# Feed-forward per 128-token block, whole-sequence loads into 64-float slots, and weights held behind the first loads, in a gated linear attention plus MLP kernel

## Chip, cores, metric

One core of one Trainium2 chip. The metric is device time in microseconds, the median of several executions. A ratio is the mean time of one kernel's fast runs over that of the other's fast runs of the same rounds, so it is not quite the ratio of the medians quoted. The profiled span is about 2 us shorter than the time.

## The reference

```python
# q, k, v, f_logit: [4, 8, 768, 48] fp32 (batch, heads, sequence, head dim)
f = 1 / (1 + exp(-f_logit))
for t in range(S):
    state = f[:, :, t, :, None] * state + einsum('bhd,bhe->bhde', k[:, :, t], v[:, :, t])
    y[:, :, t] = einsum('bhd,bhde->bhe', q[:, :, t], state)
x = y.transpose(0, 2, 1, 3).reshape(3072, 384)
h = x @ w_in                      # [384, 2048]
out = softplus(h) @ w_out         # [2048, 384]
```

The recurrence is done in 24 blocks of 128 tokens, six to a sequence.

## The kernel before

Each block of q, k, v and f_logit is loaded by itself: a partition is a token, and its 8 heads are 8 runs of 192 B in DRAM. All weights are issued early, from GpSimd (POOL), and arrive as bf16 (3.15 MB on that queue, q0 of the page).

```python
def load_qkv(i):
    t = work.tile([128, 2 * DM], FP32, name="qk", tag="qk", bufs=4)
    nc.sync.dma_start(out=t[:, 0:DM].rearrange("p (h d) -> p h d", h=H), in_=blk(q, i))
    nc.sync.dma_start(out=t[:, DM:2 * DM].rearrange("p (h d) -> p h d", h=H), in_=blk(k, i))
    ...                                            # vf likewise; load_f for f_logit
```

A block's attention is a chain: ACT makes z = log(1+exp(-f)) (`a_z`); TensorE (PE) its cumulative sum `cs`; ACT two exponentials `ee`; POOL multiplies q and k by them and casts v (`a_mul`); PE transposes (`qkT`); VectorE (DVE) copies; PE `pp`; DVE masks (`ptm`); PE `uu` (what the state gains) and `oo`; PE transposes the result into `xT`. Each engine's instructions stand in program order (in the changed kernel PE waits 4.31 us at one `uu`, until 78.94 us, and starts nothing that stands behind it); a "plan" puts each step at a tick. The feed-forward runs over pairs of blocks, 256 tokens; its second product follows LAG ticks behind.

```python
def f1(g, j):        # 16 ticks j for a pair of blocks
    for r in range(KT):                                            # KT = 3
        nc.tensor.matmul(out=hp[:, j % 2, :], lhsT=w_in_bf[:, r, j * 128:(j + 1) * 128],
                         rhs=xT[:, r, :], ...)                     # 256 columns
    # ACT: exp of two j at once, ln of four
def f2(g, j):
    for u in range(2):
        nc.tensor.matmul(out=o_ps[g][u][:, 0:DM], lhsT=g_t[g][:, j, u * T:(u + 1) * T],
                         rhs=w_out_bf[:, j, :], ...)               # 384 columns
    # after the last j: DVE adds the bias for both u (osb), SP stores; two output banks in all
```

The state's weights are 112 columns wide (`lhsT=qkp[:, NP + p, 0:112]`).

Of the kernel before, what the change touches and what calls it, by code (L numbers as in the profile page):

```python
# [15 lines left out]
LAG = 10  # L16
# [3 lines left out]
def kernel(  # L20
# [20 lines left out]
    NG = NB // 2  # L41
    GT = 2 * T
# [5 lines left out]

    nc.scalar.preload_act_table_set("natural_log_exp_and_others")


    f_t, qk_t, v_t = {}, {}, {}

    def blk(t, i):
        b, c = divmod(i, NC)
        return t[b, :, c * T:(c + 1) * T, :].rearrange("h p d -> p h d")

    def load_f(i):
        t = work.tile([128, DM], FP32, name="ff", tag="ff", bufs=4)
        nc.sync.dma_start(out=t.rearrange("p (h d) -> p h d", h=H), in_=blk(f_logit, i))  # L60
        f_t[i] = t

    def load_qkv(i):
        t = work.tile([128, 2 * DM], FP32, name="qk", tag="qk", bufs=4)
        nc.sync.dma_start(out=t[:, 0:DM].rearrange("p (h d) -> p h d", h=H), in_=blk(q, i))  # L65
        nc.sync.dma_start(out=t[:, DM:2 * DM].rearrange("p (h d) -> p h d", h=H), in_=blk(k, i))
        qk_t[i] = t
        t = work.tile([128, DM], FP32, name="vf", tag="vf", bufs=4)
        nc.sync.dma_start(out=t.rearrange("p (h d) -> p h d", h=H), in_=blk(v, i))
        v_t[i] = t  # L70

    load_f(0)
    load_qkv(0)
    load_f(1)
    load_qkv(1)


# [6 lines left out]
    WQ = 512  # L84
    for w in range(DF // WQ):
        nc.gpsimd.dma_start(
            out=w_in_bf[:, :, w * WQ:(w + 1) * WQ],
            in_=moe_w_in[:, w * WQ:(w + 1) * WQ].rearrange("(r p) n -> p r n", p=128))
    mask4 = consts.tile([128, 4, 128], BF16, name="mask4")
    for i in range(4):  # L90
        make_upper_triangular(nc, mask4[:, i, :], val=1.0, diag=True)
    last = consts.tile([128, 1], BF16, name="last")
    nc.gpsimd.tensor_copy(out=last, in_=ident[:, 127:128])
# [14 lines left out]
    for w in range(4):  # L108
        nc.gpsimd.dma_start(
            out=w_out_bf[:, 4 * w:4 * w + 4, :],  # L110
            in_=moe_w_out[512 * w:512 * (w + 1), :].rearrange("(j p) n -> p j n", p=128))
    bias_bc = consts.tile([128, DM], FP32, name="bias_bc")
# [4 lines left out]
    def emit_bias():  # L117
        ps = att_bank("biasps")
        for j in range(NJ):
            nc.tensor.matmul(out=ps[:, 0:DM], lhsT=ones, rhs=w_out_bf[:, j, :],  # L120
                             start=(j == 0), stop=(j == NJ - 1), skip_group_check=True)
        nc.vector.tensor_scalar(out=bias_bc, in0=ps[:, 0:DM], scalar1=LN2, scalar2=None,
                                op0=ALU.mult)


    z_t, cs_ps, vb_t, qkT_t, ptm_t, x_t = {}, {}, {}, {}, {}, {}
    xT_t = {}

    def a_z(i):
        ft = f_t.pop(i)  # L130
        zt = work.tile([128, DM], BF16, name="zz", tag="zz", bufs=2)
        nc.scalar.activation(out=ft, in_=ft, func=AF.Exp, bias=0.0, scale=-1.0)  # L132
        nc.scalar.activation(out=zt, in_=ft, func=AF.Ln, bias=1.0, scale=1.0)  # L133
        z_t[i] = zt

    def a_cs(i):
        ps = att_bank("cs")
        nc.tensor.matmul(out=ps[:, 0:DM], lhsT=negU, rhs=z_t.pop(i), start=True, stop=True,  # L138
                         skip_group_check=True)
        cs_ps[i] = ps  # L140

    def a_e(i):
        ps = cs_ps.pop(i)[:, 0:DM].rearrange("p (h d) -> p h d", h=H)
        et = e_bufs[i % 2]
        nc.scalar.activation(out=et[:, 0:H, 0:D], in_=ps, func=AF.Exp, bias=0.0, scale=1.0)  # L145
        nc.scalar.activation(out=et[:, H:2 * H, 0:D], in_=ps, func=AF.Exp, bias=0.0, scale=-1.0)

    def a_mul(i):
        et = e_bufs[i % 2]
        qkp = qkp_bufs[i % 3]  # L150
        nc.gpsimd.tensor_tensor(  # L151
            out=qkp[:, :, 0:D], in0=qk_t.pop(i).rearrange("p (h d) -> p h d", d=D),
            in1=et[:, :, 0:D], op=ALU.mult)
        vb = work.tile([128, DM], BF16, name="vb", tag="vb", bufs=3)
        nc.gpsimd.tensor_copy(out=vb, in_=v_t.pop(i))  # L155
        vb_t[i] = vb

    def a_tr(i):
        qkp = qkp_bufs[i % 3].rearrange("p (a b) d -> p a (b d)", b=2)
        ps = att_bank("qkT", BF16, 1024)  # L160
        for a in range(2 * NP):
# [25 lines left out]
    def a_u(i):  # L187
# [7 lines left out]
        for p in range(NP):  # L195
            nc.tensor.matmul(out=ps[0:112, 96 * p:96 * p + 96], lhsT=qkp[:, NP + p, 0:112],
                             rhs=vb[:, 96 * p:96 * p + 96], start=True, stop=True,
                             skip_group_check=True)
        for p in range(NP):
            nc.tensor.matmul(out=ps[0:112, DM + p:DM + p + 1], lhsT=ek[:, p, 0:112], rhs=last,  # L200
# [3 lines left out]
        tt = work.tile([128, NP, D], FP32, name="tt", tag="tt", bufs=2)  # L204
        for lo, e0 in ((0, 0), (64, D)):
# [6 lines left out]
        for lo, e0 in ((0, 0), (64, D)):  # L212
            hi = lo + 48
            nc.vector.tensor_tensor(out=sn[lo:hi, :, e0:e0 + D], in0=tt[lo:hi],  # L214
                                    in1=ps[lo:hi, DM:DM + NP].unsqueeze(2).to_broadcast([48, NP, D]),
# [23 lines left out]
    def a_xt(i):  # L239
        g, u = divmod(i, 2)  # L240
        if u == 0:
            xT_t[g] = work.tile([128, KT, GT], BF16, name="xT", tag="xT", bufs=2)
        xt = x_t.pop(i)
        ps = att_bank("xTp", BF16, 1024)
        for r in range(KT):
            nc.tensor.transpose(ps[:, r * 128:(r + 1) * 128], xt[:, r * 128:(r + 1) * 128], ident)  # L246
        nc.vector.tensor_copy(out=xT_t[g][:, :, u * T:(u + 1) * T],  # L247
                              in_=ps[:, 0:DM].rearrange("p (r t) -> p r t", r=KT))
# [4 lines left out]
    def f1(g, j):  # L253
        if j == 0:
            g_t[g] = work.tile([128, NJ, GT], BF16, name="gg", tag="gg", bufs=2)
        if j % 2 == 0:
# [91 lines left out]
```

## Time and profile before

| | |
|---|---|
| time, median | 223.17 us |
| span of the profiled execution | 220.7 us |
| first feed-forward matmul (T0 below) | 37.2 us |
| two blocks in the steady part | 15.0 us |

The first part of the page gives each engine's busy time and share of the span; the DMA line counts packets by size.

```profile
PE 183.1 (83%) x1792; PEld 141.4 (64%) x1792; DVE 131.7 (60%) x283; ACT 146.3 (66%) x241; POOL 59.6 (27%) x73
DMA packets 107030, 27.04 MB, mean 123 GB/s; under 512 B 100352, under 2 KB 107008, under 8 KB 107008
```

PE is the busiest engine. Of the 37.6 us that it lacks to the span, 27.3 lie before T0, where it is busy for only 9.9 us of 37.2, and 10.3 after it. The inputs are moved as nearly 100,000 packets of one 192 B run each: 24 x 4 loads x 128 tokens x 8 heads = 98,304.

### The profile page before, as it was taken

The numbers are of one execution on the slowest core, as the hardware profiler recorded it, in microseconds if no ns is written. First come the engines' busy times: TensorE is split into PE (matmuls) and PEld (weight loads), VectorE is DVE, ScalarE is ACT, GpSimd is POOL, SyncE is SP. The second block draws the span as 40 slices with busy tenths as digits, with TensorE's granted clock in tenths as the row PEclk, the third lists the DMA queues.
The fourth block names the chain that finished last, engine by engine and source line by source line (L and its number), as shares of the span: only waits on it lengthen the run. The fifth ranks groups of instructions, "written<-read, shape, count | busy, mean of one in ns | idle before, by whom it ended". The sixth has DMA issues, their size and how long they took to land.

```text
span 220.7 us, 4572 instructions
## 1 busy us (share of the span) xinstructions
PE 183.1 (83%) x1792; PEld 141.4 (64%) x1792; DVE 131.7 (60%) x283; ACT 146.3 (66%) x241; POOL 59.6 (27%) x73
## 2 busy tenths in 40 slices
PE   0022247989999989899999899899998998999992
PEld 0012135768778767677788687677876886877761
DVE  7024147677678657756776686577667766872101
ACT  4101113398798869767978687698887786867760
POOL 8920033033330232033213312331333033120000
PEclk9999999999999999999999999999999999999999
DMA  6999999996058449399394591792963851001022
GB/s 112 189 188 184 191 190 192 178 196 99 0 131 168 64 117 204 43 206 153 94 198 67 138 195 28 170 177 76 173 124 105 170 87 71 0 15 60 0 76 73
DMA packets 107030, 27.04 MB, mean 123 GB/s; under 512 B 100352, under 2 KB 107008, under 8 KB 107008
## 3 DMA queue, kind: packets, MB, share of 16 engines
q1 hardware_dynamic: 103296, 23.60, 58.2%
q0 software_dynamic: 3712, 3.15, 8.8%
q8 instruction: 14, 0.23, 0.5%
q14 instruction: 8, 0.07, 0.1%
HBM read 25.17 MB, written 4.72 MB: 135 GB/s over the span
## 4 chain that ended last, share of the span: by engine, by line
PE 68%; DVE 11%; DMA 7%; SPq 5%; issue 3%; ACT 2%; POOL 1%; DVEq 0%; POOLq 0%; ACTq 0%
PE ops L279 26%; PE hh L263 25%; DMA qk<-in_k_dram 7%; PE qkT L162 5%; DVE osb L285 3%; PE pp L179 3%; SPq L65 3%; DVE tt L210 2%; DVE sst L214 2%; PE oo L231 2%; PE xTp L246 2%; PE oo L226 1%; DVE qbd L168 1%; DVE qbd L167 1%; PE cs L138 1%
## 5 line engine op out<-in xcount | busy, mean ns | idle before, releaser
L279 PE MATMUL ops<-w_out_bf,gg 128*128 128x384 bf16 x384 | 93.3, 325 | 5.6 <-DVE osb L285 4.5
L263 PE MATMUL hh<-xT,w_in_bf 128*128 128x256 bf16 x576 | 94.2, 274 | 0.3 <-ACT uexp L268 0.2
L268 ACT ACTIVATE uexp<-hh 128x512 f32<-128x512 f32 x96 | 56.5, 589 | 28.0 <-PE hh L263 27.9
L263 PEld LDWEIGHTS <-w_in_bf 128*128 128x128 bf16 x576 | 56.1, 98 | 29.3 <-issue 3.1
L151 POOL TENSOR_TENSOR qkp<-qk,ee 128x768 bf16<-128x768 f32 x24 | 39.5, 1647 | 129.9 <-PE hh L263 62.1
L271 ACT ACTIVATE gg<-uexp 128x1024 bf16<-128x1024 f32 x48 | 50.7, 1057 | 1.5
L279 PEld LDWEIGHTS <-gg 128*128 128x128 bf16 x384 | 34.3, 98 | 11.1 <-issue 6.3
L182 DVE TENSOR_TENSOR ptm<-pp,mask 128x512 bf16<-128x512 f32 x48 | 30.8, 684 | 0.4
L236 DVE CAST xx<-oo 128x384 bf16<-128x384 f32 x24 | 13.4, 558 | 25.7 <-PE oo L231 25.7
L132 ACT ACTIVATE ff<-ff 128x384 f32<-128x384 f32 x24 | 12.2, 509 | 22.5 <-DMA ff<-in_f_logit_dram 22.5
L166 DVE COPY qkT<-qkT 128x1024 bf16<-128x1024 bf16 x24 | 16.6, 692 | 16.7 <-PE qkT L162 14.9
L162 PE MATMUL qkT<-ident,qkp 128*128 128x128 bf16 x192 | 15.9, 231 | 12.2 <-POOL qkp L151 12.2
L162 PEld LDWEIGHTS <-qkp 128*128 128x128 bf16 x192 | 12.6, 103 | 16.6 <-POOL qkp L151 16.6
L145 ACT ACTIVATE ee<-cs 128x384 bf16<-128x384 f32 x24 | 11.8, 491 | 15.2 <-PE cs L138 14.9
L247 DVE COPY xT<-xTp 128x384 bf16<-128x384 bf16 x24 | 8.6, 358 | 21.0 <-PE xTp L246 21.0
L285 DVE TENSOR_TENSOR osb<-ops,bias_bc 128x384 f32<-128x384 f32 x24 | 12.3, 553 | 13.7 <-PE ops L279 13.4
L179 PE MATMUL pp<-qbd,qkT 112*128 112x256 bf16 x96 | 15.3, 284 | 1.1 <-DVE qbd L168 1.1
L138 PE MATMUL cs<-zz,negU 128*128 128x384 bf16 x24 | 8.4, 349 | 9.1 <-ACT zz L133 9.1
L214 DVE TENSOR_TENSOR sst<-tt,uu 48x192 bf16<-48x192 f32 x40 | 14.1, 352 | 1.3
L155 POOL CAST vb<-vf 128x384 bf16<-128x384 f32 x24 | 12.1, 504 | 4.0 <-DMA vf<-in_v_dram 4.0
L133 ACT ACTIVATE zz<-ff 128x384 bf16<-128x384 f32 x24 | 12.6, 523 | 0.8
L210 DVE TENSOR_TENSOR tt<-uu,sst 48x192 f32<-48x192 f32 x32 | 11.4, 355 | 1.0
(38 smaller groups left out, 138.9 us busy)
## 6 DMA issues: line engine op xcount, KB each, us to landing
ff<-in_f_logit_dram SPq DMA_DIRECT2D x24, 192.0 KB, 4.3
qk<-in_q_dram SPq DMA_DIRECT2D x24, 192.0 KB, 4.5
qk<-in_k_dram SPq DMA_DIRECT2D x24, 192.0 KB, 4.5
vf<-in_v_dram SPq DMA_DIRECT2D x24, 192.0 KB, 4.4
out_dram<-osb SPq DMA_DIRECT2D x24, 192.0 KB, 1.9
w_in_bf<-in_moe_w_in_dram POOLq DMA_DIRECT2D x4, 384.0 KB, 9.6
w_out_bf<-in_moe_w_out_dram POOLq DMA_DIRECT2D x4, 384.0 KB, 14.7
```

Source lines behind the costliest of these rows:

```text
L151: nc.gpsimd.tensor_tensor(out=qkp[:, :, 0:D], in0=qk_t.pop(i).rearrange("p (h d) -> p h d", d=D), in1=et[:, :, 0:D], op=ALU.mult)
L162: nc.tensor.transpose(ps[:, a * 128:(a + 1) * 128], qkp[:, a, :], ident)
L166: nc.vector.tensor_copy(out=qkT, in_=pv)
L179: nc.tensor.matmul(out=ps[:, u * 256:(u + 1) * 256], lhsT=qkT[0:112, NP + p, :], rhs=qbd[0:112, p, :], start=True, stop=True, skip_group_c ...
L182: nc.vector.tensor_tensor(out=pt[:, 4 * half:4 * half + 4, :], in0=ps.rearrange("p (a t) -> p a t", t=128), in1=mask4, op=ALU.mult)
L210: nc.vector.tensor_tensor(out=tt[lo:hi], in0=uu[lo:hi, :, e0:e0 + D], in1=so[lo:hi, :, e0:e0 + D], op=ALU.add)
L214: nc.vector.tensor_tensor(out=sn[lo:hi, :, e0:e0 + D], in0=tt[lo:hi], in1=ps[lo:hi, DM:DM + NP].unsqueeze(2).to_broadcast([48, NP, D]), op ...
L263: nc.tensor.matmul(out=hp[:, j % 2, :], lhsT=w_in_bf[:, r, j * 128:(j + 1) * 128], rhs=xT[:, r, :], start=(r == 0), stop=(r == KT - 1), sk ...
L268: nc.scalar.activation(out=u_t[0][:, a:a + 2, :], in_=hp, func=AF.Exp, bias=0.0, scale=1.0)
L271: nc.scalar.activation(out=g_t[g][:, j - 3:j + 1, :], in_=u_t[0], func=AF.Ln, bias=0.5, scale=0.5)
L279: nc.tensor.matmul(out=o_ps[g][u][:, 0:DM], lhsT=g_t[g][:, j, u * T:(u + 1) * T], rhs=w_out_bf[:, j, :], start=(j == 0), stop=(j == NJ - 1 ...
L285: nc.vector.tensor_tensor(out=osb, in0=o_ps[g][u][:, 0:DM], in1=bias_bc, op=ALU.add)
```

## The change

The intent: the feed-forward starts one block after the start, not two; the state's weights get 128 columns, whose loads are shorter (in the kernel before, weight loads of 128 columns average 98 ns in the feed-forward, those of 112 columns in `uu` 143); DVE is relieved; the inputs come in a few large loads ahead of the weights. LEAD is how many ticks a block's attention begins ahead of its feed-forward.

```diff
-LAG = 10
+LAG = 30
+LEAD = 40
+    def load(name, t, b, hold=False):              # a whole sequence, six blocks
+        sb = work.tile([128, H, NC, 64], FP32, name=name, tag=name, bufs=2)
+        if hold:
+            nc.vector.memset(sb[0:1, 0, 0, 0:1], 0.0)
+        nc.sync.dma_start(
+            out=sb.rearrange("p h c d -> p (h c) d")[:, :, 0:D],
+            in_=t[b].rearrange("h (c p) d -> p (h c) d", p=T))
... # a_z takes two blocks in one instruction; a_mul: k before q, separate
+        if i == 0:
+            for w in range(4):
+                load_w_in(w)                       # w_in only behind q's product of block 0
+        if i == 1:
+            for w in range(4):
+                load_w_out(w)
... # a_u: 128 columns, state product from DVE to POOL
-            nc.tensor.matmul(out=ps[0:112, 96 * p:96 * p + 96], lhsT=qkp[:, NP + p, 0:112],
+            nc.tensor.matmul(out=ps[:, 96 * p:96 * p + 96], lhsT=qkp[:, NP + p, :],
... # f1, f2: one block, 128 columns in f1, one output bank a block
-            o_ps[g] = [psum.tile([128, 512], FP32, name="ops", tag="ops", bufs=2)
-                       for _ in range(2)]
+            o_ps[i] = psum.tile([128, 512], FP32, name="ops", tag="ops", bufs=2)
... # the plan
+        s0 = NJ * i - LEAD
+        if i % 2 == 0:
+            at(s0 - 4, a_z, i)
+    for b in range(1, B):
+        s0 = 4 if b == 1 else NJ * (NC * (b - 1) - 1) - LEAD + 4
+        at(s0, load, "ff", f_logit, b, b == 1)     # held by a memset in DVE's order
```

More of the change, by code (lines that the diff above doesn't have):

```diff
@@ L40 @@
     KT = DM // 128
-    NG = NB // 2
-    GT = 2 * T
     consts = ctx.enter_context(tc.tile_pool(name="consts", bufs=1))
@@ L47 @@
     ctx.enter_context(tc.manual_schedule())
-    nc.scalar.preload_act_table_set("natural_log_exp_and_others")
-    f_t, qk_t, v_t = {}, {}, {}
-    def blk(t, i):
-        b, c = divmod(i, NC)
-        return t[b, :, c * T:(c + 1) * T, :].rearrange("h p d -> p h d")
-    def load_f(i):
-        t = work.tile([128, DM], FP32, name="ff", tag="ff", bufs=4)
-        nc.sync.dma_start(out=t.rearrange("p (h d) -> p h d", h=H), in_=blk(f_logit, i))
-        f_t[i] = t
-    def load_qkv(i):
-        t = work.tile([128, 2 * DM], FP32, name="qk", tag="qk", bufs=4)
-        nc.sync.dma_start(out=t[:, 0:DM].rearrange("p (h d) -> p h d", h=H), in_=blk(q, i))
-        nc.sync.dma_start(out=t[:, DM:2 * DM].rearrange("p (h d) -> p h d", h=H), in_=blk(k, i))
-        qk_t[i] = t
-        t = work.tile([128, DM], FP32, name="vf", tag="vf", bufs=4)
-        nc.sync.dma_start(out=t.rearrange("p (h d) -> p h d", h=H), in_=blk(v, i))
-        v_t[i] = t
-    load_f(0)
-    load_qkv(0)
-    load_f(1)
-    load_qkv(1)
+    in_t = {}
+    def load(name, t, b, hold=False):
[5 more added lines that the diff above has]
+            in_=t[b].rearrange("h (c p) d -> p (h c) d", p=T))
+        in_t[name, b] = sb
+    load("ff", f_logit, 0)
+    load("kk", k, 0)
+    load("qq", q, 0)
+    load("vv", v, 0)
+    nc.scalar.preload_act_table_set("natural_log_exp_and_others")
     w_in_bf = consts.tile([128, KT, DF], BF16, name="w_in_bf")
@@ L83 @@
     make_identity(nc, ident)
-    WQ = 512
-    for w in range(DF // WQ):
-        nc.gpsimd.dma_start(
-            out=w_in_bf[:, :, w * WQ:(w + 1) * WQ],
-            in_=moe_w_in[:, w * WQ:(w + 1) * WQ].rearrange("(r p) n -> p r n", p=128))
     mask4 = consts.tile([128, 4, 128], BF16, name="mask4")
     for i in range(4):
-        make_upper_triangular(nc, mask4[:, i, :], val=1.0, diag=True)
+        nc.vector.tensor_scalar(out=mask4[:, i, :], in0=negU, scalar1=-1.0, scalar2=None,
+                                op0=ALU.mult)
     last = consts.tile([128, 1], BF16, name="last")
-    nc.gpsimd.tensor_copy(out=last, in_=ident[:, 127:128])
+    nc.vector.tensor_copy(out=last, in_=ident[:, 127:128])
     ones = consts.tile([128, 128], BF16, name="ones")
@@ L107, with load_w_in, load_w_out @@
         nc.vector.memset(t, 0.0)
-    for w in range(4):
+    bias_bc = consts.tile([128, DM], FP32, name="bias_bc")
+    WQ = 512
+    def load_w_in(w):
+        nc.gpsimd.dma_start(
+            out=w_in_bf[:, :, w * WQ:(w + 1) * WQ],
+            in_=moe_w_in[:, w * WQ:(w + 1) * WQ].rearrange("(r p) n -> p r n", p=128))
+    def load_w_out(w):
         nc.gpsimd.dma_start(
@@ L111, with emit_bias @@
             in_=moe_w_out[512 * w:512 * (w + 1), :].rearrange("(j p) n -> p j n", p=128))
-    bias_bc = consts.tile([128, DM], FP32, name="bias_bc")
     def att_bank(name, dt=FP32, cols=512):
         return psum.tile([128, cols], dt, name=name, tag="att", bufs=4)
-    def emit_bias():
-        ps = att_bank("biasps")
-        for j in range(NJ):
-            nc.tensor.matmul(out=ps[:, 0:DM], lhsT=ones, rhs=w_out_bf[:, j, :],
+    bias_ps = {}
+    def emit_bias(w):
+        if w == 0:
+            bias_ps[0] = att_bank("biasps")
+        for j in range(4 * w, 4 * w + 4):
+            nc.tensor.matmul(out=bias_ps[0][:, 0:DM], lhsT=ones, rhs=w_out_bf[:, j, :],
                              start=(j == 0), stop=(j == NJ - 1), skip_group_check=True)
-        nc.vector.tensor_scalar(out=bias_bc, in0=ps[:, 0:DM], scalar1=LN2, scalar2=None,
-                                op0=ALU.mult)
-    z_t, cs_ps, vb_t, qkT_t, ptm_t, x_t = {}, {}, {}, {}, {}, {}
-    xT_t = {}
+        if w == 3:
+            nc.vector.tensor_scalar(out=bias_bc, in0=bias_ps[0][:, 0:DM], scalar1=LN2,
+                                    scalar2=None, op0=ALU.mult)
+    z_t, cs_ps, vb_t, qkT_t, ptm_t, x_t, xT_t = {}, {}, {}, {}, {}, {}, {}
     def a_z(i):
-        ft = f_t.pop(i)
-        zt = work.tile([128, DM], BF16, name="zz", tag="zz", bufs=2)
+        b, c = divmod(i, NC)
+        ft = in_t["ff", b][:, :, c:c + 2, 0:D]
+        zt = work.tile([128, 2, H, D], BF16, name="zz", tag="zz", bufs=2)
         nc.scalar.activation(out=ft, in_=ft, func=AF.Exp, bias=0.0, scale=-1.0)
-        nc.scalar.activation(out=zt, in_=ft, func=AF.Ln, bias=1.0, scale=1.0)
-        z_t[i] = zt
+        nc.scalar.activation(out=zt.rearrange("p c h d -> p h c d"), in_=ft, func=AF.Ln,
+                             bias=1.0, scale=1.0)
+        z_t[i], z_t[i + 1] = zt[:, 0], zt[:, 1]
     def a_cs(i):
         ps = att_bank("cs")
-        nc.tensor.matmul(out=ps[:, 0:DM], lhsT=negU, rhs=z_t.pop(i), start=True, stop=True,
-                         skip_group_check=True)
+        nc.tensor.matmul(out=ps[:, 0:DM], lhsT=negU, rhs=z_t.pop(i).rearrange("p h d -> p (h d)"),
+                         start=True, stop=True, skip_group_check=True)
         cs_ps[i] = ps
@@ L144, in a_e @@
         et = e_bufs[i % 2]
+        nc.scalar.activation(out=et[:, H:2 * H, 0:D], in_=ps, func=AF.Exp, bias=0.0, scale=-1.0)
         nc.scalar.activation(out=et[:, 0:H, 0:D], in_=ps, func=AF.Exp, bias=0.0, scale=1.0)
-        nc.scalar.activation(out=et[:, H:2 * H, 0:D], in_=ps, func=AF.Exp, bias=0.0, scale=-1.0)
     def a_mul(i):
+        b, c = divmod(i, NC)
         et = e_bufs[i % 2]
         qkp = qkp_bufs[i % 3]
-        nc.gpsimd.tensor_tensor(
-            out=qkp[:, :, 0:D], in0=qk_t.pop(i).rearrange("p (h d) -> p h d", d=D),
-            in1=et[:, :, 0:D], op=ALU.mult)
+        k_eng = nc.vector if i == 0 else nc.gpsimd
+        k_eng.tensor_tensor(out=qkp[:, H:2 * H, 0:D], in0=in_t["kk", b][:, :, c, 0:D],
+                            in1=et[:, H:2 * H, 0:D], op=ALU.mult)
+        nc.gpsimd.tensor_tensor(out=qkp[:, 0:H, 0:D], in0=in_t["qq", b][:, :, c, 0:D],
+                                in1=et[:, 0:H, 0:D], op=ALU.mult)
+        if i == 0:
+            for w in range(4):
+                load_w_in(w)
         vb = work.tile([128, DM], BF16, name="vb", tag="vb", bufs=3)
-        nc.gpsimd.tensor_copy(out=vb, in_=v_t.pop(i))
+        nc.gpsimd.tensor_copy(out=vb.rearrange("p (h d) -> p h d", h=H),
+                              in_=in_t["vv", b][:, :, c, 0:D])
         vb_t[i] = vb
+        if i == 1:
+            for w in range(4):
+                load_w_out(w)
     def a_tr(i):
@@ L160, in a_tr @@
         ps = att_bank("qkT", BF16, 1024)
-        for a in range(2 * NP):
+        for a in list(range(NP, 2 * NP)) + list(range(NP)):
             nc.tensor.transpose(ps[:, a * 128:(a + 1) * 128], qkp[:, a, :], ident)
@@ L199, in a_u @@
         for p in range(NP):
-            nc.tensor.matmul(out=ps[0:112, DM + p:DM + p + 1], lhsT=ek[:, p, 0:112], rhs=last,
+            nc.tensor.matmul(out=ps[:, DM + p:DM + p + 1], lhsT=ek[:, p, :], rhs=last,
                              start=True, stop=True, skip_group_check=True)
@@ L204, in a_u @@
         tt = work.tile([128, NP, D], FP32, name="tt", tag="tt", bufs=2)
+        ec = work.tile([128, NP], FP32, name="ec", tag="ec", bufs=2)
+        nc.vector.tensor_copy(out=ec, in_=ps[:, DM:DM + NP])
         for lo, e0 in ((0, 0), (64, D)):
@@ L213, in a_u @@
             hi = lo + 48
-            nc.vector.tensor_tensor(out=sn[lo:hi, :, e0:e0 + D], in0=tt[lo:hi],
-                                    in1=ps[lo:hi, DM:DM + NP].unsqueeze(2).to_broadcast([48, NP, D]),
+            nc.gpsimd.tensor_tensor(out=sn[lo:hi, :, e0:e0 + D], in0=tt[lo:hi],
+                                    in1=ec[lo:hi].unsqueeze(2).to_broadcast([48, NP, D]),
                                     op=ALU.mult)
@@ L239, in a_xt @@
     def a_xt(i):
-        g, u = divmod(i, 2)
-        if u == 0:
-            xT_t[g] = work.tile([128, KT, GT], BF16, name="xT", tag="xT", bufs=2)
         xt = x_t.pop(i)
@@ L246, in a_xt, with f1 @@
             nc.tensor.transpose(ps[:, r * 128:(r + 1) * 128], xt[:, r * 128:(r + 1) * 128], ident)
-        nc.vector.tensor_copy(out=xT_t[g][:, :, u * T:(u + 1) * T],
-                              in_=ps[:, 0:DM].rearrange("p (r t) -> p r t", r=KT))
+        xT = work.tile([128, KT, T], BF16, name="xT", tag="xT", bufs=3)
+        nc.vector.tensor_copy(out=xT, in_=ps[:, 0:DM].rearrange("p (r t) -> p r t", r=KT))
+        xT_t[i] = xT
     h_ps, u_t, g_t, o_ps = {}, {}, {}, {}
-    def f1(g, j):
+    def f1(i, j):
@@ L254, in f1 @@
         if j == 0:
-            g_t[g] = work.tile([128, NJ, GT], BF16, name="gg", tag="gg", bufs=2)
-        if j % 2 == 0:
-            h_ps[0] = psum.tile([128, 2, GT], FP32, name="hh", tag="hh", bufs=2)
+            g_t[i] = work.tile([128, NJ, T], BF16, name="gg", tag="gg", bufs=4)
         if j % 4 == 0:
-            u_t[0] = work.tile([128, 4, GT], FP32, name="uexp", tag="uexp", bufs=3)
+            h_ps[0] = psum.tile([128, 4, T], FP32, name="hh", tag="hh", bufs=2)
+        if j % 8 == 0:
+            u_t[0] = work.tile([128, 8, T], FP32, name="uexp", tag="uexp", bufs=3)
@@ L260, in f1 @@
         hp = h_ps[0]
-        xT = xT_t[g]
+        xT = xT_t[i]
         for r in range(KT):
-            nc.tensor.matmul(out=hp[:, j % 2, :], lhsT=w_in_bf[:, r, j * 128:(j + 1) * 128],
+            nc.tensor.matmul(out=hp[:, j % 4, :], lhsT=w_in_bf[:, r, j * 128:(j + 1) * 128],
                              rhs=xT[:, r, :], start=(r == 0), stop=(r == KT - 1),
                              skip_group_check=True)
-        if j % 2 == 1:
-            a = j % 4 - 1
-            nc.scalar.activation(out=u_t[0][:, a:a + 2, :], in_=hp, func=AF.Exp, bias=0.0,
+        if j % 4 == 3:
+            a = j % 8 - 3
+            nc.scalar.activation(out=u_t[0][:, a:a + 4, :], in_=hp, func=AF.Exp, bias=0.0,
@@ L269, in f1, with f2 @@
                                  scale=1.0)
-        if j % 4 == 3:
-            nc.scalar.activation(out=g_t[g][:, j - 3:j + 1, :], in_=u_t[0], func=AF.Ln,
+        if j % 8 == 7:
+            nc.scalar.activation(out=g_t[i][:, j - 7:j + 1, :], in_=u_t[0], func=AF.Ln,
                                  bias=0.5, scale=0.5)
-    def f2(g, j):
+    def f2(i, j):
         if j == 0:
-            o_ps[g] = [psum.tile([128, 512], FP32, name="ops", tag="ops", bufs=2)
-                       for _ in range(2)]
-        for u in range(2):
-            nc.tensor.matmul(out=o_ps[g][u][:, 0:DM], lhsT=g_t[g][:, j, u * T:(u + 1) * T],
-                             rhs=w_out_bf[:, j, :], start=(j == 0), stop=(j == NJ - 1),
-                             skip_group_check=True)
-        if j == NJ - 1:
-            for u in range(2):
-                osb = work.tile([128, DM], FP32, name="osb", tag="osb", bufs=3)
-                nc.vector.tensor_tensor(out=osb, in0=o_ps[g][u][:, 0:DM], in1=bias_bc, op=ALU.add)
-                r0 = (2 * g + u) * T
-                nc.sync.dma_start(out=out[r0:r0 + T, :], in_=osb)
+            o_ps[i] = psum.tile([128, 512], FP32, name="ops", tag="ops", bufs=2)
+        ps = o_ps[i]
+        nc.tensor.matmul(out=ps[:, 0:DM], lhsT=g_t[i][:, j, :], rhs=w_out_bf[:, j, :],
+                         start=(j == 0), stop=(j == NJ - 1), skip_group_check=True)
+        if j == NJ - 1:
+            osb = work.tile([128, DM], FP32, name="osb", tag="osb", bufs=4)
+            nc.vector.tensor_tensor(out=osb, in0=ps[:, 0:DM], in1=bias_bc, op=ALU.add)
+            nc.sync.dma_start(out=out[i * T:(i + 1) * T, :], in_=osb)
@@ L295 @@
     for i in range(NB):
-        s0 = 8 * (i - 1) - 14
-        if i >= 2:
-            at(s0 - 16, load_f, i)
-            at(s0 - 15, load_qkv, i)
-        at(s0 - 2, a_z, i)
+        s0 = NJ * i - LEAD
+        if i % 2 == 0:
+            at(s0 - 4, a_z, i)
         at(s0, a_cs, i)
         at(s0, a_e, i)
-        at(s0 + 1, a_mul, i)
-        at(s0 + 5, a_tr, i)
-        at(s0 + 6, a_u, i)
-        at(s0 + 8, a_p, i)
-        at(s0 + 11, a_o, i)
-        at(s0 + 13, a_xt, i)
-    at(1, emit_bias)
-    NS = NG * NJ
+        at(s0 + 2, a_mul, i)
+        at(s0 + 10, a_tr, i)
+        at(s0 + 12, a_u, i)
+        at(s0 + 17, a_p, i)
+        at(s0 + 23, a_o, i)
+        at(s0 + 27, a_xt, i)
+    for b in range(1, B):
+        s0 = 4 if b == 1 else NJ * (NC * (b - 1) - 1) - LEAD + 4
+        at(s0, load, "ff", f_logit, b, b == 1)
+        at(s0 + 1, load, "kk", k, b)
+        at(s0 + 2, load, "qq", q, b)
+        at(s0 + 3, load, "vv", v, b)
+    for w in range(4):
+        at(24 + w, emit_bias, w)
+    NS = NB * NJ
     for s in range(min(plan), NS + LAG):
```

## The prediction

> **What bounds the kernel now.** I read the busy row in 40 slices first, then the rows of waits and of groups, then stretches of the timeline.
>
> ```profile
> PE   0022247989999989899999899899998998999992
> GB/s 112 189 188 184 191 190 192 178 196 99 0 131 168 64 117 204 43 206 153 94 198 67 138 195 28 170 177 76 173 124 105 170 87 71 0 15 60 0 76 73
> ```
>
> There are two regimes. For seven slices (38 us) TensorE (PE) is nearly idle and DMA runs flat at 180 to 200 GB/s; from then on PE is at 90% or more and DMA comes and goes. So the time is a start-up set by DMA, then PE's stream. The first feed-forward matmul starts at 37.2 us (T0 below) of a span of 220.7. The start-up in the chain of waits and in the timeline:
>
> ```profile
> 11.95 15.83 DMA qk<-in_k_dram
> 15.91 0.50 POOL L155 CAST vb<-vf 128x384 bf16<-128x384 f32 x1 [4.01 <-DMA vf<-in_v_dram]
> 21.20 0.52 ACT L132 ACTIVATE ff<-ff 128x384 f32<-128x384 f32 x1 [14.90 <-DMA ff<-in_f_logit_dram]
> 37.21 0.85 PE L263 MATMUL hh<-xT,w_in_bf 128*128 128x256 bf16 x3
> ```
>
> The first number is the start, the second the duration, in us. k of block 1 lands at 27.8 us, because 3.15 MB of weights share the engines with it; 9.4 us of block 1's chain follow before T0. How the sharing goes, by stretches (the last two numbers are DMA share and GB/s):
>
> ```profile
> 15.90:21.20 5.30, 1.69 (x12) 1.24 (x12) 2.71 (x6) 0.00 (x0) 0.50 (x1) 1.00 1.27 184
> 70.50:73.50 3.00, 3.00 (x33) 2.32 (x32) 1.60 (x3) 2.64 (x5) 2.09 (x2) 1.00 1.22 204
> ```
>
> With inputs alone DMA moves about 204 GB/s. Between the landings of v 0 (15.9) and f 1 (21.2) the input queue moved one tensor of 0.197 MB, 37 GB/s of 184; the weights took the rest.
>
> In the steady part a tick's matmuls are spaced by their columns:
>
> ```profile
> 104.78 0.61 PE L162 MATMUL qkT<-ident,qkp 128*128 128x128 bf16 x8
> 105.23 0.49 PE L279 MATMUL ops<-w_out_bf,gg 128*128 128x384 bf16 x2
> 105.55 0.49 PE L263 MATMUL hh<-xT,w_in_bf 128*128 128x256 bf16 x3
> 105.88 0.49 PE L279 MATMUL ops<-w_out_bf,gg 128*128 128x384 bf16 x2
> 112.73 0.36 PE L196 MATMUL uu<-vb,qkp 128*112 128x96 bf16 x4
> 112.93 0.33 PE L200 MATMUL uu<-last,ee 128*112 128x1 bf16 x4
> 113.12 0.48 PE L279 MATMUL ops<-w_out_bf,gg 128*128 128x384 bf16 x2
> ```
>
> Start to start: eight 128-column matmuls, each with its own weight load, take 0.45 us (56 ns each); two of 384 columns 0.325; three of 256 0.325. The `uu` pairs with 112-column weights take 0.39 us for eight. PE also stalls where a pair of blocks ends: both output banks wait for one DVE sum:
>
> ```profile
> 77.89 0.79 PE L279 MATMUL ops<-w_out_bf,gg 128*128 128x384 bf16 x2 [0.73 <-DVE osb L285]
> ```
>
> [...] The trace has 56 ns with loads at N=128[...]: loads of 128 columns average 98 ns, of 112 columns 143. [...] An input packet is 192 B, a w_out row in bf16 768 B[...], and the trace has 37 of 184. [...]
>
> **The change part by part.**
>
> *First product per 128 tokens.* 576 matmuls of 109.2 ns (62.9 us) become 1152 of 55.8 (64.3 us): +1.4 us. The doubled loads hide, as in the transposes. The second product keeps 384 matmuls of 162.5 ns, 62.4 us.
>
> *uu padded to 128 columns.* 0.39 us becomes about 0.27 (4 x 42.5 by columns, 4 x 25 as the 48-column pairs of `oo` show), 20 times: -2.4 us.
>
> *PE's stream.* Attention per block: cs 0.16, qkT 0.45, pp 0.44, oo 0.17 + 0.21, xTp 0.17, uu 0.27 x 5/6: 1.83. With 5.28 of feed-forward 7.1 us, x24 = 170.8, plus bias 2.6: 173.4 us after, some 174.3 before.
>
> *Stalls at pair ends.* Before, six blocks take 45.05 us (74.86 to 119.91, the same copy in the chain), 7.51 each against 7.15 of stream: 0.36 a block, some 8 us in all. After, each block has one output bank while the other has been free for a whole block, the state product goes from DVE to POOL (2 x 0.352 us a block), and the attention leads by 40 ticks. I expect nearly all of it gone: -7 us. Load per block: ACT 6.3 us (4 x 0.589 + 2 x 1.057 + 2 x 0.49 + half of two 768-wide passes of about 0.84), DVE about 5.3, POOL about 3.1. None exceeds 7.1.
>
> *Start-up.* One load is now 1.18 MB, 5.8 us at 204 GB/s. Data flows from 1.7 us: f ends at 7.5, k 13.2, q 18.9 (lands 19.7). POOL multiplies q (half of 1.65 us) and issues w_in from 20.6; its data starts near 21.8. v is then half done, 0.57 MB to go, at about 35 GB/s against 1 KB weight rows. Both together: (0.57 + 1.57)/188 GB/s = 11.4 us. So **v lands at about 34.2 us**. PE's queue holds uu 0 ahead of pp 0, so everything waits for v. Then, from landing: POOL vb 0.5; PE uu, DVE ec and two tt to 2.2; POOL state products to 3.2, k and q products of block 1 to 4.9, vb to 5.4; PE transposes to 6.0 (at the slow early pace, 1.03 for eight); DVE qkT and qbd to 7.55, xT 7.9, ec and tt 8.8, ptm 10.1; PE oo 1, then the first feed-forward matmul at 10.3. **T0 = 44.5 us**, 7.3 later than now.
>
> *After T0.* PE has 173.4 - 3.6 (blocks 0 and 1) = 169.8 us left. For 30 ticks the second product isn't there yet and ACT is the limit: 12 us of ACT and 1 to fill against 11 of PE, +2; the slow pace again +1; POOL, held 3 us by issuing w_out, +0.7; v of the second sequence lands near 74, needed near 74.5, +0.5. End: osb and store 3.4 (3.9 now).
>
> *Sum*: 44.5 + 169.8 + 4.2 + 3.4 = 221.9 us of span against 220.7. The profiled run took 1.8 us more than its span: 223.7. About 7 us gained in the steady part, 7 lost at the start.
>
> **The rivals.** *A, loads become the bound*[...]. Against it: the 56 ns above and the 26 ns spacing of 48-column pairs. 4%. *B, start-up shorter than I think*: if aligned slots or longer transfers lift the rate to 260 GB/s, v and w_in are in by about 28 us and T0 is 38: 217. For it: the layout looks built for that, and 228 GB/s appear in the first microsecond. [...] Or v gets more than 1 in 6 beside w_in; then w_in is late instead. *C, start-up longer, or a new wait*: all of a sequence must land before its first v is used; at 175 GB/s T0 is 48 and the second sequence's v stalls PE too, some 230. Stores queue behind 1.18 MB loads in SP's queue; I count four osb buffers as just enough (store 1 done near 97, its buffer wanted at 100). *D, the stalls stay* because DVE's order still matters: +5, 229.
>
> **Range and chances.** The main term is T0 (plus or minus 4), then the stalls (plus or minus 4). I take 0.7 off for B's alignment: 223 us, 215 to 231. Within 2% (218.7 to 227.6) 0.55; faster 0.25, mostly B; slower 0.20, from A, C, D.
>
> **What would show it.** The 128-column hh triples spaced 167 ns (A wrong)[...]; uu groups 0.27 us; six blocks in about 42.8 us and no wait of ops for osb; v landing near 34 and the first hh near 44.5; ACT-ended waits of PE in the 12 us after it. If hh starts before 40, my sharing or rate is wrong; if the steady period is above 7.3 us, an engine I called slack isn't.

Some of these figures are estimates; this is what the traces have beside them. The times of one matmul, 109.2, 55.8, 162.5 and 42.5 ns for 256, 128, 384 and 96 columns: start to start, the kernel before has 0.325 us for three of 256, 0.45 for eight of 128, 0.325 for two of 384 and 0.17 for four of 96 (`oo`, 102.93 to 103.10 us), that is 108, 56, 162.5 and 42.5 ns. The 35 GB/s of v beside w_in and the share of 1 in 6, here and in the expectation of e1: the kernel before has 37 of 184 GB/s, beside w_out. The 260 GB/s of rival B is an assumption: over stretches of 2 us or more, the highest rate read in any run is 233 (e3, 36 to 40 us). Of rival C, the changed kernel's trace shows stores behind loads in SP's queue: the first output sum is made at 64.0 us, its store is issued at 82.9, behind loads of f and k.

## The result

The changed kernel takes 230.35 us (230.25 to 231.08), the kernel before 222.82 us on the same chip: ratio 1.0336, 95% interval 1.0289 to 1.0383. It is **slower by 3.4%**. The time lies inside the stated range, near its end, and on the side that was given 0.20.

The same rows of the page, for the changed kernel:

```profile
PE   0001127888999299999999999999999999999994
PEclk9999999999999979999999999999999999999999
GB/s 111 163 164 163 163 185 167 201 174 168 150 176 166 167 165 168 190 164 214 126 165 158 154 165 185 98 34 35 3 37 39 34 4 34 39 39 34 37 34 69
DMA packets 32026, 27.10 MB, mean 119 GB/s; under 512 B 768, under 2 KB 32000, under 8 KB 32000
```

Three things are new. DMA starts at 163 GB/s, not at 180 to 190. The packets are a third in number: 24,576 of them now carry four runs, 768 B (98,304 / 4; with 3,072 store rows and 3,584 weight rows that makes the 31,232 between 512 B and 2 KB). And there is a hole in PE in slice 14, with a lower clock in slice 15.

The start-up in the timeline (start, duration, engine, line; in brackets the idle time before and what ended it):

```profile
10.61 0.84 ACT L129 ACTIVATE ff<-ff 128x768 f32<-128x768 f32 x1 [8.59 <-DMA ff<-in_f_logit_dram]
17.92 0.56 DVE L151 TENSOR_TENSOR qkp<-kk,ee 128x384 bf16<-128x384 f32 x1 [11.56 <-DMA kk<-in_k_dram]
25.20 0.91 POOL L153 TENSOR_TENSOR qkp<-qq,ee 128x384 bf16<-128x384 f32 x1 [23.39 <-DMA qq<-in_q_dram]
32.17 0.50 POOL L159 CAST vb<-vv 128x384 bf16<-128x384 f32 x1 [2.87 <-DMA vv<-in_v_dram]
41.58 1.13 PE L271 MATMUL hh<-xT,w_in_bf 128*128 128x128 bf16 x9
```

The row of busy times from 26 to 30 us, where POOL issues w_in (the last number is GB/s): the rate is still that of one load alone, so v gets nearly all of it.

```profile
26.00:30.00 4.00, 0.60 (x4) 0.45 (x5) 1.44 (x3) 0.00 (x0) 3.30 (x5) 1.00 1.13 164
```

Each sequence load takes some 7.3 us (1.18 MB at 163 GB/s); v lands at 32.2 us, and T0 is 9.4 us later, at 41.6: 4.4 us later than before. From T0 to the end it takes 186.9 us, before 183.5. So both parts lost. Inside the second part the stream itself is better:

```profile
95.46 0.33 PE L271 MATMUL hh<-xT,w_in_bf 128*128 128x128 bf16 x3
95.63 0.33 PE L286 MATMUL ops<-w_out_bf,gg 128*128 128x384 bf16 x1
95.79 0.33 PE L271 MATMUL hh<-xT,w_in_bf 128*128 128x128 bf16 x3
```

The three 128-column matmuls take 0.165 us from start to start, 55 ns each; a tick of one block costs 0.33 us as predicted. Six blocks take 43.8 us (the qkT copies at 116.53 and 160.31), before 45.05. What eats that gain again is in two places. First, the timeline of PE near 75 us, and PE's row for 79.0 to 82.6 us (the third number from the right is the granted clock):

```profile
74.30 0.33 PE L271 MATMUL hh<-xT,w_in_bf 128*128 128x128 bf16 x3
78.94 0.35 PE L204 MATMUL uu<-vb,qkp 128*128 128x96 bf16 x4 [4.31 <-POOL vb L159]
79.51 0.53 PE L271 MATMUL hh<-xT,w_in_bf 128*128 128x128 bf16 x3
79.83 0.53 PE L286 MATMUL ops<-w_out_bf,gg 128*128 128x384 bf16 x1
```

```profile
79.00:82.60 3.60, 3.60 (x29) 2.58 (x29) 0.78 (x3) 1.22 (x2) 1.00 (x2) 0.53 1.12 163
```

The v of the second sequence lands at 78.4 us; POOL's cast and PE's `uu` stand behind it. PE is idle for 4.3 us; counted from 74.47, when the next matmul would have started, the loss is 4.5 us. Then a triple takes 0.32 us, twice the time, for 3.4 us: another 1.7 us, with 0.53 of the clock granted over that row. In the packed traces the slow stretches last 3.41 us here, 6.83 in e4 and 10.24 in e2 (mean granted clock 0.993, 0.985 and 0.976).

Second, the waits (the three numbers are the total in us, how often, and the longest in us):

```profile
PE cs L136 <- ACT zz L130: 16.0, 11, 12.4
```

Without the longest, at the start, these are ten waits of 0.36 us on average, one for nearly every later pair of blocks: ACT's two passes over a pair (0.84 us each) come too late for the cumulative sum.

### The profile page after: what moved, and what is told of

Same layout as the page of the kernel before. It is cut to its first block, busy times and chain, and to the rows that moved or that the text cites. A ratio compares the mean times of both kernels' runs of the same rounds, so it can differ in the third digit from the quotient of the medians.

```text
span 228.5 us, 5679 instructions
## 1 busy us (share of the span) xinstructions
PE 182.9 (80%) x2368; PEld 148.3 (65%) x2368; DVE 120.3 (53%) x270; ACT 143.3 (63%) x217; POOL 80.2 (35%) x127
## 4 chain that ended last, share of the span: by engine, by line
PE 52%; DMA 19%; SPq 13%; ACT 7%; POOL 4%; DVE 2%; issue 1%; DVEq 0%; POOLq 0%
PE ops L286 21%; PE hh L271 19%; DMA vv<-in_v_dram 14%; SPq L55 13%; DMA out_dram<-osb 5%; PE pp L187 3%; PE qkT L170 3%; ACT zz L130 3%; ACT ff L129 2%; ACT uexp L276 2%; PE cs L136 2%; PE oo L241 1%; POOL w_out_bf L103 1%; PE oo L236 1%; PE uu L204 1%
## 5 line engine op out<-in xcount | busy, mean ns | idle before, releaser
L271 PE MATMUL hh<-xT,w_in_bf 128*128 128x128 bf16 x1152 | 125.6, 221 | 0.5 <-ACT uexp L276 0.5
L286 PE MATMUL ops<-w_out_bf,gg 128*128 128x384 bf16 x384 | 121.1, 328 | 0.0
L271 PEld LDWEIGHTS <-w_in_bf 128*128 128x128 bf16 x1152 | 95.9, 99 | 26.3 <-issue 1.6
L224 POOL TENSOR_TENSOR sst<-tt,ec 48x192 bf16<-48x192 f32 x40 | 20.1, 503 | 55.1 <-DVE tt L220 45.3
L151 POOL TENSOR_TENSOR qkp<-kk,ee 128x384 bf16<-128x384 f32 x23 | 21.0, 913 | 35.5 <-ACT ee L143 35.3
L153 POOL TENSOR_TENSOR qkp<-qq,ee 128x384 bf16<-128x384 f32 x24 | 21.9, 914 | 23.4 <-DMA qq<-in_q_dram 23.4
L170 PEld LDWEIGHTS <-qkp 128*128 128x128 bf16 x192 | 12.4, 102 | 25.8 <-DVE qkp L151 17.1
L290 DVE TENSOR_TENSOR osb<-ops,bias_bc 128x384 f32<-128x384 f32 x24 | 13.4, 558 | 22.2 <-PE ops L286 20.1
L246 DVE CAST xx<-oo 128x384 bf16<-128x384 f32 x24 | 13.4, 557 | 7.3 <-PE oo L241 6.9
L129 ACT ACTIVATE ff<-ff 128x768 f32<-128x768 f32 x12 | 10.0, 836 | 8.6 <-DMA ff<-in_f_logit_dram 8.6
L204 PE MATMUL uu<-vb,qkp 128*128 128x96 bf16 x80 | 7.2, 217 | 10.3 <-POOL vb L159 10.3
L159 POOL CAST vb<-vv 128x384 bf16<-128x384 f32 x24 | 12.1, 503 | 8.6 <-DMA vv<-in_v_dram 8.6
L204 PEld LDWEIGHTS <-qkp 128*128 128x128 bf16 x80 | 5.3, 105 | 10.5 <-issue 10.5
```

Source lines behind the costliest of these rows:

```text
L151: k_eng.tensor_tensor(out=qkp[:, H:2 * H, 0:D], in0=in_t["kk", b][:, :, c, 0:D], in1=et[:, H:2 * H, 0:D], op=ALU.mult)
L153: nc.gpsimd.tensor_tensor(out=qkp[:, 0:H, 0:D], in0=in_t["qq", b][:, :, c, 0:D], in1=et[:, 0:H, 0:D], op=ALU.mult)
L170: nc.tensor.transpose(ps[:, a * 128:(a + 1) * 128], qkp[:, a, :], ident)
L224: nc.gpsimd.tensor_tensor(out=sn[lo:hi, :, e0:e0 + D], in0=tt[lo:hi], in1=ec[lo:hi].unsqueeze(2).to_broadcast([48, NP, D]), op=ALU.mult)
L271: nc.tensor.matmul(out=hp[:, j % 4, :], lhsT=w_in_bf[:, r, j * 128:(j + 1) * 128], rhs=xT[:, r, :], start=(r == 0), stop=(r == KT - 1), sk ...
L286: nc.tensor.matmul(out=ps[:, 0:DM], lhsT=g_t[i][:, j, :], rhs=w_out_bf[:, j, :], start=(j == 0), stop=(j == NJ - 1), skip_group_check=True)
```

## The experiments

In all of them the result was correct. Times beside the changed kernel's 230.35 and the kernel before, run with each batch (222.9 to 223.2).

| run | time, us | ratio to before | T0, us |
|---|---|---|---|
| changed kernel | 230.35 | 1.0336 | 41.6 |
| e1 dense rows | 221.91 | 0.9954 | 38.2 |
| e2 loads per block | 216.91 | 0.9724 | 24.8 |
| e3 no hold | 225.30 | 1.0103 | 41.7 |
| e4 ACT pair earlier | 228.85 | 1.0261 | 41.8 |
| e5 = e1 + e3 + e4 | 217.90 | 0.9760 | 38.0 |
| e6 weights first | 240.65 | 1.0790 | 51.3 |
| e7 small loads, LEAD 32 | 209.17 | 0.9333 | 19.6 |
| e8 small loads, LEAD 40 | 211.28 | 0.9463 | 21.8 |
| e9 e5, 112 columns | 219.58 | 0.9837 | 38.3 |
| e10 e5, state product on DVE | 219.66 | 0.9843 | 40.4 |
| e11 compute parts alone | 217.25 | 0.9737 | 38.7 |
| e12 best: e7, w_out split | 207.22 | 0.9285 | 20.0 |

### e1: dense rows

```diff
-        sb = work.tile([128, H, NC, 64], FP32, name=name, tag=name, bufs=2)
+        sb = work.tile([128, H, NC, D], FP32, name=name, tag=name, bufs=2)
```

> The changed kernel with whole-sequence loads into dense rows of 48 floats, no 64-float slots. Measured with slots: packets of 768 B, 163 GB/s with inputs alone, f/k/q/v of the first sequence at 10.6, 17.9, 25.2, 32.2 us, second v at 78.4. Theory (slots changed the packets, and with them rate and sharing): packets go back to 192 B, the rate to about 204 GB/s, q lands near 20, v near 34 since it again gets only a sixth beside the weights, second v near 74; about 226 us. Rival (the length of the transfer sets the rate, slots do nothing): 163 GB/s and 230 us again.

221.91 us. Both theories fell. The page counts exactly the same packets as with slots, so the slots did not make them; but the rate did change. The same stretch, inputs alone, with slots and then without:

```profile
12.00:20.00 8.00, 1.09 (x5) 0.35 (x4) 0.56 (x1) 1.20 (x3) 0.00 (x0) 1.00 1.12 163
```

```profile
12.00:20.00 8.00, 1.00 (x5) 0.34 (x4) 0.56 (x1) 0.87 (x2) 0.00 (x0) 1.00 1.08 186
```

POOL's cast of the first v in the timeline without slots, with its wait for the load in brackets:

```profile
28.79 0.50 POOL L159 CAST vb<-vv 128x384 bf16<-128x384 f32 x1 [1.83 <-DMA vv<-in_v_dram]
```

186 GB/s against 163: **the 64-float slots, which looked like alignment, cost an eighth of the load rate**, and that accounts for the 8.4 us gained: T0 comes 3.4 us earlier, the second v stops PE for 0.9 us and not for 4.5 (3.6), and the clock dip (1.7) is gone; 8.7 in all. Why a strided destination slows these transfers, no run shows. (The narrower row also moves the tiles in memory, which no run tells apart from the gap.) No run loads single blocks into slots.

163 GB/s is not the most that DMA gives, either. In e3, where slotted loads run beside those of w_in, the two together move 233 GB/s, by the packed trace 102 of inputs and 131 of w_in:

```profile
36.00:40.00 4.00, 3.14 (x26) 2.18 (x26) 2.85 (x8) 1.16 (x3) 4.00 (x7) 1.00 1.17 233
```

### e2: one load per block

```diff
-        sb = work.tile([128, H, NC, 64], FP32, name=name, tag=name, bufs=2)
... # one load for six blocks
+            sb = work.tile([128, H, 48], FP32, name=name, tag=name, bufs=4)
+            nc.sync.dma_start(out=sb[:, :, 0:D], in_=src(t))
... # src: block i, 8 runs of 192 B; no hold any more
```

> The changed kernel with one load per block of 128 tokens (dense on the DRAM side as before, 64-float slots on chip, four buffers), all else as changed, weights still held behind block 0. Theory (the loss is the whole-sequence loads: the first v at 32 us, and the second v late): T0 falls from 41.6 to about 25, some waiting for blocks 2 and 3 until about 31, no wait of PE for v later; about 209 us. Rival (the loss is in the per-block feed-forward, its doubled weight loads or its dependences): T0 may fall but the stretch from 116 to 160 us keeps its waits and the whole stays above 222.

The edit that ran is not the one expected: its rows are dense, 48 floats, so it undoes the slots and the large loads at once. It must be compared with e1, whose rows are dense too.

216.91 us: T0 24.8 as expected, and 13.4 us gained, not 21. The packets are 192 B again (98,304 of the 100,352 under 512 B), and beside w_out they starve:

```profile
41.62 0.84 ACT L128 ACTIVATE ff<-ff 128x768 f32<-128x768 f32 x1 [6.95 <-DMA ff<-in_f_logit_dram]
43.38 0.48 PE L135 MATMUL cs<-zz,negU 128*128 128x384 bf16 x1 [6.52 <-ACT zz L129]
```

So f of blocks 4 and 5 lands at 41.6 us, PE stands for 6.5 us, and the clock dips again. Against e1 the smaller loads bring the start forward by 13.4 us (T0 38.2 to 24.8), and 5.0 us reach the time (221.91 to 216.91); the hold is gone with the large loads, which this pair of runs does not separate. So the first half of the theory holds, and the rival is refuted. The size of the gain was missed because I had only counted waits until 31 us.

### e3: no hold

```diff
+    load("ff", f_logit, 1)          # straight behind load("vv", v, 0); kk, qq, vv likewise
-    for b in range(1, B):
-        s0 = 4 if b == 1 else NJ * (NC * (b - 1) - 1) - LEAD + 4
+    for b in range(2, B):
+        s0 = NJ * (NC * (b - 1) - 1) - LEAD + 4
```

> The changed kernel with the loads of the second sequence issued straight behind those of the first, without the hold. Theory (the second v arriving at 78.4 costs 4.3 us of idle PE and then 1.8 us of slow clock): v lands before 72, both vanish, PE busy in the stretch where it waited; about 6 us less, 224 us, if w_in is not delayed by more than 1 or 2 us. Rival: beside the weights the early loads delay w_in and w_out, T0 or the bias wait moves out by as much, 229 to 231 us.

225.30 us. PE's wait for v and the dip are gone (mean clock 0.998, not 0.993); T0 moved by 0.1, and PE waited 1.4 us for w_out at the bias. 4.5 + 1.7 - 1.4 = 4.8 of the 5.05 gained. The hold, meant to keep early loads away from the weights, was worth less than the lateness it caused.

### e4: the ACT pair 8 ticks ahead

```diff
-            at(s0 - 4, a_z, i)
+            at(s0 - 8, a_z, i)
```

> The changed kernel with the pair of sigmoid-log passes on ACT planned 8 ticks ahead of the cumulative sum, not 4. Theory (ten waits of PE for zz, 3.6 us in all after the first): they vanish, two blocks take 14.25 us, not 14.6; about 3.5 us less, 227 us. Rival: ACT's order shifts and the same time is lost in waits of hh for uexp; 230 us.

228.85 us, 1.5 less and not 3.5. The waits for zz are gone except the first, and two blocks take 14.25 us (14.6 in the changed kernel), so the mechanism is right. But the second v comes when DMA brings it:

```profile
PE uu L204 <- POOL vb L159: 10.9, 2, 5.7
```

The row of busy times for 80 to 82 us of the same run, its columns as above:

```profile
80.00:82.00 2.00, 2.00 (x14) 1.41 (x12) 0.78 (x3) 0.01 (x1) 1.01 (x2) 0.50 1.11 162
```

PE arrives earlier at `uu` and so waits longer, 5.2 us (10.9 less the 5.7 at the start) and not 4.4, and works at half clock until 85.5 us, 6.0 us long and not 3.4. Upstream of this wait for a transfer the gain was worth nothing; it even cost 1.3 us of clock (half of the 2.6 us more).

### e5: the three undone together

> Three causes undone together: dense rows (alone 8.4 us better than the changed kernel), no hold on the second sequence (alone 5.0 better), the ACT pair 8 ticks ahead (alone 1.5 better). Theory (slots and hold both act through the late second v, so they overlap; the ACT pair's 3.6 us of waits are worth more once no wait for v swallows them): dense 221.9, less 0.9 of v wait left there, less 3.5 of zz waits: 217.5 us. Rival (the three simply add): 230.35 - 8.4 - 5.0 - 1.5 = 215.4 us.

The edit is e1, e3 and e4 in one. 217.90 us: the theory's 217.5, not the rival's 215.4. Dense rows and the hold act through the same late v, so they don't add. The granted clock is 1.000, no wait for zz or the second v is left, and six blocks take 42.8 us (105.93 to 148.72), 7.13 each. This is the changed kernel's compute and load shape without its three faults: 2.4% faster than the kernel before.

### e6: weights first

```diff
-        if i == 0:                       # in a_mul
-            for w in range(4):
-                load_w_in(w)             # w_out at i == 1 likewise
+    for w in range(4):                   # at the start, ahead of all else on POOL
+        load_w_in(w)
+    for w in range(4):
+        load_w_out(w)
```

> The changed kernel with both weights issued at the start, ahead of everything on POOL, as the kernel before has them. Theory (holding the weights back is what keeps the start at 41.6 us): with 3.15 MB beside 4.7 MB of inputs, about half the engines each until the weights are in, v lands near 44 and T0 is near 53; 240 us, and the clock goes slow less because PE waits less later. Rival (total bytes until block 0 are nearly the same, since w_in is needed anyway): v lands near 40, T0 near 47, 234 us.

240.65 us. Half the engines each is an estimate; in e3 the inputs get 102 of 233 GB/s beside w_in. In the timeline v lands, and the feed-forward begins, 10 us later than in the changed kernel:

```profile
41.84 0.50 POOL L161 CAST vb<-vv 128x384 bf16<-128x384 f32 x1 [5.74 <-DMA vv<-in_v_dram]
51.26 1.13 PE L270 MATMUL hh<-xT,w_in_bf 128*128 128x128 bf16 x9
```

So the hold on the weights is a good part of the change, worth 10.3 us once the first loads are this large.

### e9 and e10: the compute parts, one at a time

```diff
# e9, on e5
-            nc.tensor.matmul(out=ps[:, 96 * p:96 * p + 96], lhsT=qkp[:, NP + p, :],
+            nc.tensor.matmul(out=ps[0:112, 96 * p:96 * p + 96], lhsT=qkp[:, NP + p, 0:112],
# (the ek matmuls and ec likewise)
# e10, on e5
-            nc.gpsimd.tensor_tensor(out=sn[lo:hi, :, e0:e0 + D], in0=tt[lo:hi],
+            nc.vector.tensor_tensor(out=sn[lo:hi, :, e0:e0 + D], in0=tt[lo:hi],
```

> The kernel of the three undone causes (217.9 us, two blocks in 14.2 us) with the state weights back to 112 columns. Theory (eight uu pairs take 0.39 us with 112 columns and 0.27 with 128): 20 blocks times 0.12, 2.4 us more, 220.3. Rival (the weight loads hide behind neighbours anyway): no difference, 217.9.

219.58 us, 1.7 more than e5. In e9's timeline, then in e5's:

```profile
136.45 0.36 PE L208 MATMUL uu<-vb,qkp 128*112 128x96 bf16 x4
136.84 0.32 PE L290 MATMUL ops<-w_out_bf,gg 128*128 128x384 bf16 x1
```

```profile
135.06 0.33 PE L208 MATMUL uu<-vb,qkp 128*128 128x96 bf16 x4
135.33 0.32 PE L290 MATMUL ops<-w_out_bf,gg 128*128 128x384 bf16 x1
```

0.39 us against 0.27 from the first uu to the next other matmul, exactly as reckoned. Of the 20 x 0.12 = 2.4 us, 1.7 show in the time. In the steady part too six blocks, with five such groups, take 43.25 us (107.09 to 150.34 in the qkT copies) against 42.8, 0.09 us a group and not 0.12; where the rest is made up, no run shows.

> The same base with the two state products back on DVE. Theory (the stalls at pair ends of the kernel before went away because each block has one output bank and the other is free; DVE's order has slack now): DVE 0.7 us busier a block, no wait of PE for osb, 218 us. Rival (moving the products to POOL is what freed DVE's order): PE waits for osb or ptm again, some 0.3 us a block, 224 us.

219.66 us, and the theory holds: six blocks take 42.8 us (114.94 to 157.73 in the qkT copies), as in e5, with DVE at 136.0 us of work and not 120.5, and PE never waits for osb. So it is not the unburdened DVE that ended the stalls at pair ends. That leaves the separate output bank a block, or the longer LAG and LEAD, which changed with it; no run takes the bank back alone. The 1.8 us lie at the start, where DVE's chain is on the path: T0 is 40.4 and not 38.0. (The intervals of the ratios of e9 and e10 don't overlap that of e5, 0.9723 to 0.9797, so both losses are clear of noise.)

### e11: the compute parts alone

The edit is e2, e6 and e4 in one: loads and weights as the kernel before has them, and the ACT pair 8 ticks ahead.

> The compute parts of the change alone: the changed kernel with loads per block (dense, as the kernel before) and both weights issued at the start, as the kernel before; the ACT pair 8 ticks ahead. Theory (the compute parts are a gain of about 0.4 us a block, hidden in the changed kernel by its loads): T0 about 33, then 7.1 us a block; 212 us. Rival (the loads of 192 B starve beside both weights so long that nothing is gained at the start and block 2 waits): 220 us.

217.25 us, 2.6% faster than the kernel before, but not 212: T0 is 38.7, where I expected 33. The steady part is as expected (six blocks in 42.8 us). What I had missed is that `a_z` takes two blocks in one instruction, so nothing starts before f of block 1 is in, and that stands behind the weights:

```profile
22.90 0.48 PE L140 MATMUL cs<-zz,negU 128*128 128x384 bf16 x1 [22.90 <-ACT zz L134]
```

In the kernel before the first `cs` runs at 4.9 us.

### e7, e8, e12: a version that beats both

```diff
-LAG = 30
-LEAD = 40
+LAG = 48
+LEAD = 32            # e8: 44 and 40; e12: 48 and 36
+            sb = work.tile([128, 2, H, D], FP32, name=name, tag=name, bufs=3)
+            for u in range(2):                   # one load per block, order f, k, q, v by pairs
+                nc.sync.dma_start(out=sb[:, u], in_=t[b, :, (c + u) * T:(c + u + 1) * T, :]
+                                  .rearrange("h p d -> p h d"))
-            at(s0 - 4, a_z, i)
+            at(s0 - 8, a_z, i)
-        if i == 1:
-            for w in range(4):
+        if i == 2:                               # e12: if i in (2, 4):
+            for w in range(4):                   #          for w in range(i - 2, i):
```

> An attempt at a version that beats both: the changed compute with per-block loads (dense, two per pair of blocks, 192 B packets), ACT pair 8 ticks ahead, LEAD 32 and LAG 48, w_out held until block 2's products. Theory (with small first loads T0 is about 17 to 20 us, and then DMA limits until about 42 us, when weights and three pairs are in): PE waits some 12 us in all between 20 and 45, then two blocks in 14.25 us; 203 us. Rival (192 B packets starve beside w_out, about 37 GB/s, and a lead of 32 ticks leaves no slack, so PE waits every block): 213 us or more.

> The same with LEAD 40 and LAG 44. Theory: T0 is some 3 us later because block 1's attention is ahead of it in PE's queue, and block 2's data is waited for sooner; the same bytes end the DMA-bound part, so 203 to 206 us. Rival (lead is what the steady part needs): faster than LEAD 32 by several us, its two blocks 14.25 us where LEAD 32 has more than 15.

209.17 and 211.28 us: e7 lies between its theory and its rival, e8 above its theory and no faster than e7. T0 is 19.6 and 21.8. Both keep two blocks at 14.2 us, so LEAD 40 buys nothing in the steady part, and the rival of e8 is refuted. These two kernels spread more than the others (e7 206.7 to 211.8; its profiled execution was the slowest; the median of 209.17 includes it, the ratio doesn't). The clock of their profiled executions is 0.973 and 0.982, with PE waits in the first 46 us.

> The best version so far (LEAD 32, 209.2 us) with w_out released in two halves, behind the products of blocks 2 and 4, LEAD 36 and the bias 12 ticks later. In the best version PE waits 4.7 us near 41 to 46 for q of the third pair, which stands behind w_out. Theory: that wait shrinks to 2 us and the clock stays up; 206 us. Rival (bytes needed by then are the same, so the wait moves to the second half of w_out): 209 us.

207.22 us, ratio 0.9285 (0.9235 to 0.9335). The wait for q of the third pair is gone, and one for the second half of w_out has come in its place, smaller:

```profile
PE qkT L167 <- POOL qkp L150: 2.2, 4, 1.6
PE biasps L114 <- DMA w_out_bf<-in_moe_w_out_dram: 2.2, 1, 2.2
```

The interval of e7's ratio (0.9261 to 0.9406) overlaps e12's, so that e12 is better than e7 is likely but not shown. That e12 beats both the kernel before and the changed one is.

## Why the prediction was right or wrong

The range held the time, by 0.65 us; the point, 223, and the most likely verdict, "within 2%", did not. That it held is partly luck, since large errors in T0 cancel. By its own steps:

- **PE's stream: right.** The 128-column triples are spaced 165 ns (167 said), uu takes 0.27 us, and where no wait intrudes a block takes 7.13 us (7.1 said): e5, e10, e11. Rival A is dead; their weight loads, 99 ns each on average in the changed kernel, hide.
- **Stalls at pair ends: right.** No wait of PE for osb is left. Of the three reasons given, e10 rules out the state product's move to POOL; between the output banks and the longer lead it stays open.
- **T0: 44.5 said, 41.6 measured**, from three errors that partly cancel. The rate was taken as 204 GB/s, from loads of one block; it was 163, so q lands at 25.2 and not at 19.7: +5.5. Then v was said to need 14.5 us more, because it shares with w_in; it took 7.0, which is what a load takes alone: -7.5. The chain behind v took 9.4, not 10.3: -0.9. The sharing hardly took place. POOL issues w_in from 26.05, but in the packed trace its first packet moves at 30.4, 4.4 us later and not 1.2, when v has about 0.1 MB to go (the row for 26 to 30 us above). So rival B's last form, w_in late, is what happened. Why it starts so late is open (2.3 us after the issue in the kernel before). The share of 1 in 6 was an estimate; with 192 B packets the kernel before has 37 of 184 GB/s, and where 768 B packets do overlap with w_in, in e3, inputs get 102 of 233. The sign "if hh starts before 40, my sharing or rate is wrong" did not appear, though both were wrong.
- **"v of the second sequence lands near 74, needed near 74.5, +0.5": the step that failed most.** It was needed at 74.5, as said, and landed at 78.4, because of the same 163 GB/s. The cost was 4.5 us of standing and 1.7 of slow clock, 6.2 in place of 0.5. e3 took it away for 5.05 us; e1, by the rate alone, cut the standing to 0.9. I had named it under rival C, at 175 GB/s, and gave C too little; C's "some 230" came true, but its T0 of 48 did not.
- **"None exceeds 7.1": wrong as an argument.** ACT's 6.3 us a block is below PE's 7.1, but its order put the pair's two passes, 1.7 us, and often a `uexp` of 0.6, into four ticks of 0.45 us (`uexp` is the exponential of a product `hh`). 0.36 us a pair, 3.6 in all, against nothing in the sum. e4 took the waits away.
- **"I take 0.7 off for B's alignment": the wrong way.** The slots brought no gain; they lost 12% of the rate (163 GB/s against 186 without them, e1), and that I had not allowed for.

The sum then: 221.9 us of span predicted; T0 -2.9, second v +5.7, zz +3.6 make 228.3; measured 228.5. That it closes does not show every other term right, but e5, which has neither the late v nor the waits for zz, takes 177.9 us from T0 to the end, where the prediction's terms without its 0.5 for v make 176.9. The largest term, the second v, comes from the load rate, and e1, which changes nothing but the row length of the tile, brings the kernel back to a ratio of 0.9954.

What stays open: why the strided rows slow the 768 B packets, why w_in's data starts late, what ended the stalls at pair ends, and where the few tenths between the sums and the measurements are.

## What to carry to other kernels

In this kernel a load's form went with its packet size, its rate and its share beside another queue: measure the rate of the very form (stretch, bytes, row length) before a plan is built on another's. Size alone did not bring rate: loads of 0.197 MB in 192 B packets ran at 187 GB/s (e2, 6 to 9 us) to 204 (the kernel before, 70.5 to 73.5 us), loads of 1.18 MB in 768 B packets at 186 (e1, 12 to 20 us), in 64-float slots at 163. A transfer that was just in time by a reckoning on paper was a wait of 4.5 us plus 1.7 of slow clock here, so leave some microseconds of room, or cut it smaller so that the first piece comes early. Busy times below the bound's period don't exclude waits: check that the work fits between the ticks where it stands.
